# Linear attention times a gated layer, on one core: a key operand stored instead of formed late, two last stores moved to another queue, and small steps of the moments moved to ScalarE

## The chip, the cores and the metric

The kernel runs on one core of a Trainium2 chip. The metric is the device time in microseconds of one execution. The core has TensorE (PE; PEld is its weight load), VectorE (DVE), ScalarE (ACT), GpSimd (POOL) and SyncE (SP). In this kernel SyncE only issues transfers, and GpSimd issues transfers besides computing. Each engine works through its own queue in order; an instruction that waits holds everything behind it on its engine.

## The reference, cut to what matters

```python
xn = layernorm(x)                       # x: 2048 x 1024, eps 1e-5
q, k, v = split(xn @ wqkv)              # 32 heads of 32
phi = lambda t: where(t > 0, t + 1, exp(t)) + 1e-6
kv = einsum("hsd,hse->hde", phi(k), v);  z = sum_s phi(k)
o = (phi(q) @ kv) / (phi(q) @ z + 1e-6)
s = o @ wo
g = silu((silu(xn @ w1) * (xn @ w3)) @ w2)      # 1024 -> 3584 -> 1024
out = x + s * g
```

All of it is float32. The kernel never forms v. It forms the matrix xn^T phi(k), called G here, and multiplies that by the weights of v.

## The kernel before

**Products.** Every large product is cut into a 2 x 2 scheme with seven half-size products in place of eight, so each operand appears in seven forms: four quarters or less, and sums or differences of quarters (S1 to S4, T1 to T4). Each form is split in two parts, a high one (ScalarE, line 95) and the rest (VectorE, line 96), and each product of two forms is three matmuls (lines 103 to 105). A form therefore costs a pass of ScalarE and a pass of VectorE before TensorE can use it.

**The order.** `half(0)` and `half(1)` (lines 654 to 727) take 1024 rows of x each. A half normalises its rows and turns them into the seven left forms, then makes the keys (four pairs of 128 x 2 columns), the queries, and gate and up of the gated layer. After them come the attention product and the second product of the gated layer, in segments; the last segment finishes the output (`finish`, line 1191). The code is unrolled. A planner sets the order of the instructions on each engine from their order in the code, their operands' readiness and the free buffers by its own model of time; a few places hold it with `issue_after`, which puts instructions of a block behind a given one on that one's engine.

**The head of the first half.** The first chunk is 512 rows, four tiles of 128 x 1024 (`xa`). For each, `moments` (line 132) takes VectorE's batch statistics and `spread` (line 143) makes mean and 1/sqrt(variance + eps): one root on ScalarE, everything else in tiny VectorE steps of one or two columns. VectorE normalises the tile in place (line 157), and TensorE turns it. The second chunk (`xb`, line 191) has its moments two tiles at a time. For each of its tiles `prepare_rest` (line 201) normalises it on VectorE, then GpSimd forms S1, S3, S2 and S4 of both chunks, one after the other (lines 212 to 215), and stores them (line 217), and TensorE turns five forms, S2 and S4 from the first chunk's tile among them. The products T2 x S2 and after need the forms of all four tiles. Of the early key products, `gemm(..., early=True)` (line 432), only the two that need the quarters of the first chunk come before.

**The keys.** For each pair, `key_rows` (line 519) applies phi to the four quarters of the result; `turn` (line 532), called three steps of the surrounding products later, transposes them and forms the right operands Y00, Y01, Y10, R5, R4 and R2 of a later product, each 128 x 512, and stores them to DRAM (`keep_keys`, line 516, on GpSimd's queue). Y00, c21, c22, c12 and R2 come from one pool of six buffers (`small`, line 116).

**The row products.** In the second half, after its keys and queries, `row_products` (line 558) forms G: seven products, listed in `ROWS`, each summed over four pieces of 256 rows, so 28 steps. A step loads two tiles of x_d (SyncE, line 572) and two of y_d (line 570) into one of two `raw` buffers, splits them, and runs 24 matmuls. The seventh product needs R2 - Y00: it loads Y00 into an extra tile `yy` (from the four `job` buffers) and GpSimd subtracts it in place (line 583). The same `job` buffers serve side work that runs along: the denominators (line 841) and the division of the queries (`divide`, line 872, loads on lines 882 and 884).

**The end.** The last segment's `tokens` (line 1039) finish four quarters (t, n) of each of eight groups of 256 rows, in the order (1,1), (0,0), (1,0), (0,1). `finish` loads the factor s (and x), applies silu on ScalarE, multiplies, adds x and stores through GpSimd's queue. For rows with t = 1, except in the last group, the store adds to x in DRAM.

Of the kernel before, what the change touches and what calls it, by code (L numbers as in the profile page):

```python
# [16 lines left out]
P = 128  # L17
C = 512
# [4 lines left out]
def tile_linear_attention_times_swiglu(  # L23
# [32 lines left out]
    eps = const.tile([P, 1], F32, name="tiny")  # L56
    nc.vector.memset(eps, 1e-6)
    hmask = const.tile([P, P], F32, name="hmask")
    nc.vector.memset(hmask, 0.0)
# [24 lines left out]
    XS = ["A11", "A12", "S1", "S3", "A22", "S2", "S4"]  # L84
    YS = ["Y00", "Y01", "Y10", "R5", "R2", "R4"]
    x_d = [dram.tile([P, TH // 2, len(XS), C], F32, name=f"x_d{h}") for h in range(NH)]
# [44 lines left out]

    def moments(xs, dst):

        bs = st.tile([P, 2, 2, nc.vector.BN_STATS_DIM], F32, tag="bs", name="bs")
        for c, t in enumerate(xs):
            gather(t, bs[:, c])
        spread(bs, dst)

    def gather(t, bs):
# [3 lines left out]
    def spread(bs, dst):  # L143
        n = dst.shape[1]
        v, y, u = (st.tile([P, 2], F32, tag=a, name=a)[:, :n] for a in "vyu")
        for c in range(n):
            nc.vector.bn_aggr(out=dst[:, c], in_=bs[:, c])
        nc.vector.tensor_scalar_add(v, dst[:, :, 1], 1e-5)
        nc.scalar.activation(y, v, AF.Sqrt)
        nc.vector.reciprocal(y, y)  # L150

        nc.vector.tensor_mul(u, y, y)
        nc.vector.scalar_tensor_tensor(u, u, -0.5, v, op0=ALU.mult, op1=ALU.mult)
        nc.vector.scalar_tensor_tensor(dst[:, :, 1], u, 1.5, y, op0=ALU.add, op1=ALU.mult)

    def normalise(t, m):
# [19 lines left out]
    def prepare_first(A, mom):  # L176

        xs = []
        for g in range(TH // 4):
            t = load_rows([(2 * g + e) * P for e in range(2)], f"xa{g}")  # L180
            xs += [t[:, e] for e in range(2)]
            for i in (2 * g, 2 * g + 1):
                moments(xs[i:i + 1], mom[:, i:i + 1])
                normalise(xs[i], mom[:, i])
                keep_rows(0, i, "A11", xs[i])
                turn_into(A, {"A11": xs[i][:, :C]}, i, f"0_{i}")
        for i, t in enumerate(xs):
# [12 lines left out]

    def prepare_rest(A, mom, i, t0, seconds, behind):

        with ExitStack() as order:
# [4 lines left out]
            t1, s1 = seconds[i], small(f"S1x{i}")  # L208
            normalise(t1, mom[:, TH // 2 + i])

# [308 lines left out]
    def key_rows(h, pair):  # L519
# [12 lines left out]
        def turn(n, c, pk):  # L532
            V = nc.vector
            p_ = turned(pk, f"k{h}_{pair}_{n}{c}")
            if (c, n) == (0, 0):
                y00 = small(f"y00_{h}_{pair}")
                nc.scalar.activation(y00, p_, AF.Identity, bias=eps)  # L537
# [10 lines left out]
            else:  # L548
# [4 lines left out]
                for n_, t in (("Y01", y01), ("R4", r4), ("R2", r2)):  # L553
                    keep_keys(h, pair, n_, t)

        return use

    def row_products():
# [5 lines left out]
        def load(i, h, t):  # L564
            x_, y_, less = ROWS[i]
            raw = praw.tile([P, 4, C], F32, tag="raw", name=f"xy{i}_{h}{t}")

            def rows(dst, n):
                src = y_d[h][:, t:t + 2, YS.index(n)].rearrange("p t j d -> p t (j d)")
                nc.sync.dma_start(out=dst, in_=src)  # L570

            nc.sync.dma_start(out=raw[:, :2], in_=x_d[h][:, t:t + 2, XS.index(x_)])
            rows(raw[:, 2:], y_)
            other = None
            if less:
                other = job_tile([P, 2, C], f"yy{i}_{h}{t}")
                rows(other, less)
            return raw, other

        def ready(i, h, t):  # L580
            raw, other = data[i, h, t]
            if other is not None:
                nc.gpsimd.tensor_sub(out=raw[:, 2:], in0=raw[:, 2:], in1=other)
            out = []
            for e in range(2):
# [12 lines left out]
        for at, s in enumerate(steps):  # L598
# [25 lines left out]

    ROWS = [("A22", "Y10", None), ("A12", "Y00", None), ("S2", "R2", None), ("S1", "R4", None),
            ("S3", "R5", None), ("S4", "Y01", None), ("A11", "R2", "Y00")]

# [562 lines left out]

    def finish(m, t, n, a):
        r0, cols = (2 * m + t) * P, slice(n * C, (n + 1) * C)
        ss = small(f"ss{m}_{t}{n}")
        nc.sync.dma_start(out=ss, in_=s_d[2 * m + t][:, cols])
        if not added_by_dma(m, t):
            xs = small(f"xs{m}_{t}{n}")
            nc.sync.dma_start(out=xs, in_=x[r0:r0 + P, cols])
        nc.scalar.activation(a, a, AF.Silu)
        nc.vector.tensor_mul(a, a, ss)
        if not added_by_dma(m, t):  # L1200
            nc.vector.tensor_add(a, a, xs)
            nc.gpsimd.dma_start(out=out[r0:r0 + P, cols], in_=a)
        else:
# [98 lines left out]
```

## Time and profile before

| | us |
|---|---|
| median of 3 runs | 2360.43 (2357.89 to 2363.99) |
| the profiled execution, its own time | 2364.7 |
| its span, first to last instruction | 2362.9 |
| TensorE busy in the span | 2306.2 |
| VectorE, ScalarE, GpSimd busy | 1775.7, 924.5, 697.2 |
| mean granted TensorE clock | 0.992 |

The execution's own time is 1.8 us more than its span; this lies around the first and last instruction. A row of a timeline gives start, duration, engine, line, operation, output and inputs, how many were merged, and in brackets the idle time of the engine before it with what ended it. A row of the waits gives who waited, for whom, the total in us, how often, and the longest. A row of the windows gives the stretch, its length, the busy us of PE, PEld, DVE, ACT and POOL with the number of instructions, the granted clock, the DMA share and GB/s. `SPq` and `POOLq` are the issue of a transfer or a wait in that engine's queue.

### The profile page before, as it was taken

How to read it: one execution, taken by the hardware profiler on the slowest of the kernel's cores; microseconds unless marked ns; L12 is line 12 of the kernel's file. 1: busy time of each engine (PE TensorE's matmuls, PEld its weight loads, DVE VectorE, ACT ScalarE, POOL GpSimd, SP SyncE). 2: the span in 40 equal slices, each digit the busy share in tenths (PEclk: the TensorE clock that was granted, in tenths of full speed). 3: DMA queues.
4: the chain of work that ended last, by engine and by line, in shares of the span. 5: the costliest groups of instructions: out<-in, count | busy, mean ns of one | idle time of the engine just before them, and what ended most of it. 6: DMA issues, size and time to landing. Idle time of an engine off the chain costs nothing.

```text
span 2362.9 us, 30966 instructions
## 1 busy us (share of the span) xinstructions
PE 2306.2 (98%) x10368; PEld 1893.2 (80%) x10368; DVE 1775.7 (75%) x2822; ACT 924.5 (39%) x1639; POOL 697.2 (30%) x852
## 2 busy tenths in 40 slices
PE   6999999999999999998999999999999999999998
PEld 5788878888887888776888888888887788888876
DVE  8887888898877775656867688887745666767798
ACT  5555343423232555433233332334324534342433
POOL 5120433377866111012423435342310000000033
PEclk9999999999999999999999999999999999999999
DMA  6555455576669546776665567665756565766688
GB/s 236 165 174 178 156 179 183 172 228 220 225 210 321 196 134 205 255 257 207 201 193 181 188 200 218 195 216 168 230 153 195 181 198 172 225 208 182 191 265 260
DMA packets 354015, 479.69 MB, mean 203 GB/s; under 512 B 24144, under 2 KB 262736, under 8 KB 353744
## 3 DMA queue, kind: packets, MB, share of 16 engines
q1 hardware_dynamic: 316608, 359.20, 48.1%
q0 software_dynamic: 37248, 118.52, 15.2%
q8 instruction: 81, 1.33, 0.2%
q14 instruction: 78, 0.64, 0.1%
HBM read 308.81 MB, written 172.49 MB: 204 GB/s over the span
## 4 chain that ended last, share of the span: by engine, by line
PE 74%; DMA 5%; DVE 5%; issue 2%; ACT 1%; SPq 1%; POOL 0%; DVEq 0%; POOLq 0%; ACTq 0%
PE g L103 2%; PE g L104 2%; PE g L105 2%; PE cB L103 1%; PE cB L104 1%; PE cB L105 1%; PE dB L103 1%; PE dB L104 1%; PE dB L105 1%; PE aB L105 1%; PE aB L103 1%; PE aB L104 1%; DMA rA12B<-h_d 1%; PE bB L105 1%; PE bB L103 1%
## 5 line engine op out<-in xcount | busy, mean ns | idle before, releaser
L756 POOL DMA_DIRECT2D h_d<-sg x112 | 82.7, 739 | 262.5 <-DVE sg L752 183.9
L1069 POOL DMA_DIRECT2D u_d<-uB x32 | 17.3, 541 | 407.9 <-DVE uB L1052 354.8
L96 DVE TENSOR_TENSOR xy<-xy,xy 128x512 fp32r<-128x512 f32 x112 | 75.0, 704 | 70.4 <-ACT xy L95 70.2
L95 ACT CAST xy<-xy 128x512 fp32r<-128x512 f32 x112 | 65.1, 620 | 109.3 <-PE g L105 62.5
L103 PE MATMUL g<-xy,xy 128*128 128x512 f32 x224 | 82.3, 403 | 7.1 <-ACT xy L95 7.1
L104 PE MATMUL g<-xy,xy 128*128 128x512 f32 x224 | 88.5, 395 | 0.0
L105 PE MATMUL g<-xy,xy 128*128 128x512 f32 x224 | 87.9, 393 | 0.0
L517 POOL DMA_DIRECT2D y_d<-y x40 | 28.6, 718 | 141.9 <-ACT y L537 81.6
L1052 DVE TENSOR_TENSOR acc<-cB,acc 128x512 f32<-128x512 f32 x50 | 34.4, 688 | 40.2 <-PE cB L105 40.2
L1052 DVE TENSOR_TENSOR acc<-dB,acc 128x512 f32<-128x512 f32 x56 | 38.5, 688 | 31.0 <-PE dB L105 30.8
L736 POOL TENSOR_TENSOR hs<-hs,sg 128x256 f32<-128x256 f32 x56 | 61.1, 1090 | 0.1
L103 PEld LDWEIGHTS g<-xy,xy 128*128 128x128 f32 x224 | 42.1, 190 | 21.9 <-ACT xy L95 9.6
L738 POOL TENSOR_TENSOR hs<-sg 128x256 f32<-128x256 f32 x56 | 57.7, 1031 | 0.0
L894 POOL DMA_DIRECT2D qs_d<-qd x32 | 18.0, 564 | 119.3 <-DVE qd L890 82.0
L1183 POOL DMA_DIRECT2D s_d<-s x32 | 17.3, 541 | 117.7 <-DVE s L1052 70.9
L735 POOL TENSOR_TENSOR hs<-sg,sg 128x256 f32<-128x256 f32 x56 | 50.8, 906 | 1.2
L104 PEld LDWEIGHTS g<-xy,xy 128*128 128x128 f32 x224 | 42.7, 190 | 9.9 <-issue 0.8
L739 POOL TENSOR_TENSOR hs<-sg,hs 128x256 f32<-128x256 f32 x56 | 49.9, 892 | 1.5
L105 PEld LDWEIGHTS g<-xy,xy 128*128 128x128 f32 x224 | 42.6, 190 | 9.2
L771 POOL TENSOR_TENSOR w<-w 128x256 f32<-128x256 f32 x28 | 28.2, 1006 | 70.9 <-DMA w<-in_B_w 69.7
L764 POOL DMA_DIRECT2D h_d<-hs x60 | 45.8, 765 | 4.3 <-POOL hs L739 2.4
L674 POOL DMA_DIRECT2D pq_d<-pq x32 | 17.5, 546 | 91.1 <-DVE pq L507 88.3
(5315 smaller groups left out, 8330.1 us busy)
## 6 DMA issues: line engine op xcount, KB each, us to landing
h_d<-hs POOLq DMA_DIRECT2D x60, 256.0 KB, 3.5
h_d<-sg POOLq DMA_DIRECT2D x56, 256.0 KB, 3.9
w<-in_B_w SPq DMA_DIRECT2D x56, 256.0 KB
wt_d<-w SPq DMA_DIRECT2D x28, 512.0 KB
xy<-x_d SPq DMA_DIRECT2D x28, 512.0 KB
xy<-y_d SPq DMA_DIRECT2D x28, 512.0 KB
h_d<-hs SPq DMA_DIRECT2D x52, 256.0 KB
qs_d<-qd POOLq DMA_DIRECT2D x32, 384.0 KB, 3.9
```

The source lines that it names most:

```text
L95: nc.scalar.copy(out=hi, in_=src)
L96: return nc.vector.tensor_sub(out=lo, in0=src, in1=hi.bitcast(F32))
L103: nc.tensor.matmul(acc, lhsT=wh, rhs=ah, start=start, stop=False, skip_group_check=True)
L104: nc.tensor.matmul(acc, lhsT=wh, rhs=al, start=False, stop=False, skip_group_check=True)
L105: return nc.tensor.matmul(acc, lhsT=wl, rhs=ah, start=False, stop=stop, skip_group_check=True)
L735: e.tensor_add(out=s1, in0=a21, in1=a22)
L736: e.tensor_sub(out=s2, in0=s1, in1=a11)
L738: e.tensor_sub(out=s3, in0=a11, in1=a21)
L739: e.tensor_sub(out=s4, in0=a12, in1=s2)
L756: nc.gpsimd.dma_start(out=h_d[i][2 * h + c][:, 2 * n:4 * n + 2, k], in_=src)
L764: queue.dma_start(out=h_d[i][2 * h + c][:, 6 + 4 * e:10 + 4 * e, k], in_=o[e].rearrange("p (e s) -> p e s", s=P))
L1052: return V.tensor_add(out=c, in0=src, in1=c)
```

## The change

It has three parts.

1. In `key_rows`, Y00's tile is kept; when R2 is formed, VectorE overwrites it with R6 = R2 - Y00, and it is stored as a seventh key operand. `ROWS` names R6 for the seventh product; the `yy` load and GpSimd's subtraction go.
2. In the last group of rows, the stores of (1,0) and (0,1) are issued by SyncE, the others by GpSimd as before. A new `fetch` holds the loads of `finish`; in the last group the loads for (0,1) are issued with those of (1,0), ahead of its store.
3. In the first half, each tile has moments of its own (`settle`). VectorE keeps the statistics, their aggregate and the reciprocal; ScalarE makes the one-column steps: six with the root for a tile of the first chunk, eight for one of the second, where it also forms minus mean times the scale, and then normalises the tile in one pass. The first chunk's tiles are still normalised by VectorE, and the second half's rows are left as they are.

```diff
+    few = const.tile([P, 2], F32, name="few")
+    nc.vector.memset(few[:, 0:1], 1e-5)
+    nc.vector.memset(few[:, 1:2], 1.5)
...
-    YS = ["Y00", "Y01", "Y10", "R5", "R2", "R4"]
+    YS = ["Y00", "Y01", "Y10", "R5", "R2", "R4", "R6"]
...
+    def settle(bs, m, shift):
+        v, y, u = (st.tile([P, 2], F32, tag=a, name=a) for a in "vyu")
+        def act(out, src, **how):
+            nc.scalar.activation(out, src, AF.Identity, **how)
+        mean, r = m[:, 0:1], m[:, 1:2]
+        nc.vector.bn_aggr(out=m, in_=bs)
+        act(v[:, :1], r, bias=few[:, 0:1])
+        nc.scalar.activation(y[:, :1], r, AF.Sqrt, bias=few[:, 0:1])
+        nc.vector.reciprocal(y[:, :1], y[:, :1])
+        act(u[:, :1], y[:, :1], scale=y[:, :1])
+        act(u[:, :1], u[:, :1], scale=v[:, :1])
+        act(u[:, :1], u[:, :1], scale=-0.5, bias=few[:, 1:2])
+        act(r, u[:, :1], scale=y[:, :1])
+        if shift:
+            act(u[:, 1:], mean, scale=r)
+            act(mean, u[:, 1:], scale=-1.0)
...
-                moments(xs[i:i + 1], mom[:, i:i + 1])
+                bs = st.tile([P, 2, nc.vector.BN_STATS_DIM], F32, tag="bs", name="bs")
+                gather(xs[i], bs)
+                settle(bs, mom[:, i], False)
                 normalise(xs[i], mom[:, i])
...
-        moments(ts, mom[:, j:j + 2])
+        for e, t in enumerate(ts):
+            bs = st.tile([P, 2, nc.vector.BN_STATS_DIM], F32, tag="bs", name="bs")
+            gather(t, bs)
+            settle(bs, mom[:, j + e], True)
...
-            normalise(t1, mom[:, TH // 2 + i])
+            m1 = mom[:, TH // 2 + i]
+            nc.scalar.activation(t1, t1, AF.Identity, scale=m1[:, 1:2], bias=m1[:, 0:1])
...
-                y00 = small(f"y00_{h}_{pair}")
+                y00 = rows["y00"] = small(f"y00_{h}_{pair}")
...
+                V.tensor_sub(out=rows["y00"], in0=r2, in1=rows["y00"])
+                keep_keys(h, pair, "R6", rows["y00"])
...
-            other = None
-            if less:
-                other = job_tile([P, 2, C], f"yy{i}_{h}{t}")
-                rows(other, less)
-            return raw, other
+            return raw
...
-            if other is not None:
-                nc.gpsimd.tensor_sub(out=raw[:, 2:], in0=raw[:, 2:], in1=other)
...
-            ("S3", "R5", None), ("S4", "Y01", None), ("A11", "R2", "Y00")]
+    ROWS = [("A22", "Y10"), ("A12", "Y00"), ("S2", "R2"), ("S1", "R4"), ("S3", "R5"), ("S4", "Y01"), ("A11", "R6")]
...
+    factors = {}
+    def fetch(m, t, n):
         r0, cols = (2 * m + t) * P, slice(n * C, (n + 1) * C)
-        ss = small(f"ss{m}_{t}{n}")
+        ss, xs = small(f"ss{m}_{t}{n}"), None
         nc.sync.dma_start(out=ss, in_=s_d[2 * m + t][:, cols])
         if not added_by_dma(m, t):
             xs = small(f"xs{m}_{t}{n}")
             nc.sync.dma_start(out=xs, in_=x[r0:r0 + P, cols])
+        factors[m, t, n] = ss, xs
+
+    def finish(m, t, n, a):
+        r0, cols = (2 * m + t) * P, slice(n * C, (n + 1) * C)
+        if (m, t, n) not in factors:
+            fetch(m, t, n)
+        if (m, t, n) == (NG - 1, 1, 0):
+            fetch(m, 0, 1)
+        ss, xs = factors[m, t, n]
+        queue = nc.sync if m == NG - 1 and t != n else nc.gpsimd
         nc.scalar.activation(a, a, AF.Silu)
         nc.vector.tensor_mul(a, a, ss)
         if not added_by_dma(m, t):
             nc.vector.tensor_add(a, a, xs)
-            nc.gpsimd.dma_start(out=out[r0:r0 + P, cols], in_=a)
+            queue.dma_start(out=out[r0:r0 + P, cols], in_=a)
```

More of the change, by code (lines that the diff above doesn't have):

```diff
@@ L130, in load_rows @@
         return t
[L132 to L137, printed above, removed]
     def gather(t, bs):
@@ L564, in load @@
         def load(i, h, t):
-            x_, y_, less = ROWS[i]
+            x_, y_ = ROWS[i]
             raw = praw.tile([P, 4, C], F32, tag="raw", name=f"xy{i}_{h}{t}")
@@ L573, in load @@
             rows(raw[:, 2:], y_)
-            other = None
-            if less:
-                other = job_tile([P, 2, C], f"yy{i}_{h}{t}")
-                rows(other, less)
-            return raw, other
+            return raw
         def ready(i, h, t):
-            raw, other = data[i, h, t]
-            if other is not None:
-                nc.gpsimd.tensor_sub(out=raw[:, 2:], in0=raw[:, 2:], in1=other)
-            out = []
+            raw, out = data[i, h, t], []
             for e in range(2):
@@ L623, in row_products @@
             del data[s]
-    ROWS = [("A22", "Y10", None), ("A12", "Y00", None), ("S2", "R2", None), ("S1", "R4", None),
-            ("S3", "R5", None), ("S4", "Y01", None), ("A11", "R2", "Y00")]
+    ROWS = [("A22", "Y10"), ("A12", "Y00"), ("S2", "R2"), ("S1", "R4"), ("S3", "R5"), ("S4", "Y01"), ("A11", "R6")]
     def row_sums(i, m, b, u, v):
@@ L1189, in added_by_dma @@
         return m < ADDED and t == 1
-    def finish(m, t, n, a):
+    factors = {}
+    def fetch(m, t, n):
         r0, cols = (2 * m + t) * P, slice(n * C, (n + 1) * C)
-        ss = small(f"ss{m}_{t}{n}")
+        ss, xs = small(f"ss{m}_{t}{n}"), None
         nc.sync.dma_start(out=ss, in_=s_d[2 * m + t][:, cols])
```

## The prediction

> **What bounds the kernel now.** I read the page's busy shares first, then the list of who waits for whom on TensorE, then the table of windows, then the timelines of the places that the waits point to.
>
> ```profile
> PE 2306.2 (98%) x10368; PEld 1893.2 (80%) x10368; DVE 1775.7 (75%) x2822; ACT 924.5 (39%) x1639; POOL 697.2 (30%) x852
> ...
> PE tA L164 <- DVE v L148: 11.2, 1, 11.2
> PE g L103 <- ACT xy L95: 7.1, 2, 6.9
> PE bk__735 L103 <- ACT S L95: 4.7, 1, 4.7
> PE tS L164 <- DVE pk L507: 2.9, 1, 2.9
> ...
> 40.00:50.00 10.00, 5.70 (x30) 4.70 (x28) 9.96 (x13) 4.53 (x9) 9.89 (x11) 0.80 0.49 200
> ...
> 1080.00:1090.00 10.00, 4.34 (x10) 3.47 (x11) 2.59 (x4) 2.28 (x4) 2.33 (x1) 0.68 0.73 204
> ```
>
> TensorE is busy 98% of the span (first row), so what can be won is where it stands still. The rows of waits give engine, what was awaited, us in total, times, longest. The long ones lie in two places that the change touches: the head (11.2, 4.7, 2.9) and one step of the row products (6.9). The window rows give PE, PEld, DVE, ACT, POOL busy of 10 us, then the granted clock, which falls to 0.80 and 0.68 just there: a pause is paid twice, once as idle time and once as slow matmuls behind it. Outside these places TensorE never stops for long, so microseconds won there should reach the end.
>
> **Part 1, R2 - Y00 stored as R6.** The last four of the 28 steps of the row products lose a 512 KB load and a GpSimd subtraction each. The last step is the one that TensorE waited for:
>
> ```profile
> 1067.34 3.25 SPq L884 DMA_DIRECT2D qd<-pq_d  x1
> ...
> 1072.40 1.07 SPq L570 DMA_DIRECT2D xy<-y_d  x1
> ...
> 1082.63 2.33 POOL L583 TENSOR_TENSOR xy<-xy,yy 128x1024 f32<-128x1024 f32 x1 [8.67 <-DMA xy<-y_d]
> ...
> 1085.66 2.07 PE L103 MATMUL g<-xy,xy 128*128 128x512 f32 x4 [6.87 <-ACT xy L95]
> ...
> 1093.48 0.39 PE L103 MATMUL ag__9096<-A,B11g__9047 128*128 128x512 f32 x1
> 1093.71 0.39 PE L104 MATMUL ag__9096<-A,B11g__9047 128*128 128x512 f32 x1
> ...
> SPq L882 <- POOL xy L583: 3.8, 1, 3.8
> ...
> y_d<-r POOLq DMA_DIRECT2D x8, 256.0 KB, 3.4
> ```
>
> The chain reads backwards: TensorE starts the step at 1085.66 after 6.87 us, because GpSimd subtracts for 2.33 us from 1082.63, because the keys issued at 1072.40 land only then, 10 us later. That issue is late since SyncE's queue holds loads of the division (L882, L884) ahead of it, which in turn waited 3.8 us for the subtraction to give back `job` buffers, and those loads share the DMA engines with it. The step's 24 matmuls take 1085.66 to 1093.48, 7.82 us; at the 0.23 us between the two rows of `ag` they take 5.5. So the stall costs 6.87 + 2.3 = 9.2 us.
>
> With R6 stored no `yy` holds a `job` buffer, so the division's loads go out earlier, as the denominators' four free up, ahead of the last step's loads. Four loads of 512 KB are gone, though the division's take part of that room. The last step's `raw` buffer comes free when the step two before it is split, which waits for no subtraction any more. If only the 3.25 us of L884 go ahead of them, the keys are issued at 1069.2; landing in 7 us (an estimate between the 3.4 that a store of half the size takes, last row, and the 10.2 here) they are there at 1076.2, and the first operand 0.7 us later (1082.63 + 2.33 to 1085.66), before 1078.79, where TensorE stood still. I take -9.2. Bounds: -10.2, if the weight behind it comes earlier too, and -2.3, if the loads stay late and only the subtraction goes.
>
> What R6 adds is eight subtractions and eight 256 KB stores, one per key pair:
>
> ```profile
> 101.25 0.68 DVE L507 SCALAR_TENSOR_TENSOR pk<-c12k__1007,pk 128x512 f32<-128x512 f32 x1
> ...
> 103.13 0.68 DVE L552 SCALAR_TENSOR_TENSOR r<-trk,y 128x512 f32<-128x512 f32 x1
> ...
> 125.43 0.81 POOL L517 DMA_DIRECT2D y_d<-r  x1
> ...
> 100.00:120.00 20.00, 20.00 (x101) 16.57 (x100) 17.09 (x35) 11.47 (x21) 5.75 (x8) 1.00 0.52 159
> ```
>
> Eight times 0.68 is 5.4 us of VectorE and eight times 0.81 is 6.5 of GpSimd. In the key windows VectorE has 2.9 us in 20 free and GpSimd 14, and TensorE never pauses, so this hides; uncovered it would be 5.4. There is a new wait: R6 overwrites Y00's tile, so VectorE must wait until Y00's store has read it; behind it in VectorE's queue stand the additions of the next product. Two products lie between (24 matmuls, 5.5 us), and a store takes 0.8 + 3.4. And Y00's tile stays held. In the first half four pairs make Y00 early, the last at:
>
> ```profile
> 88.86 0.68 ACT L537 ACTIVATE y<-trk,tiny 128x512 f32<-128x512 f32 x1
> ```
>
> From there to about 108 (R2's row, 0.8 to issue and 3.4 to land after it), four of the six small buffers are Y00s, and c22, c21, c12 and R2 live on two. By their rows they overlap by at most two (c12 is read by 101.9, R2 is born at 103.1, the first two rows), so it just fits. I put +1.0 for both (0 to 5.4).
>
> **Part 2, the head.** For the second chunk VectorE makes moments and normalises while GpSimd sums:
>
> ```profile
> 21.24 3.65 DVE L141 BATCH_NORM_STATS2 bs<-xb 128x6 f32<-128x512 f32 x6
> ...
> 28.25 0.16 DVE L153 SCALAR_TENSOR_TENSOR u<-u,v 128x2 f32<-128x2 f32 x1
> ...
> 30.79 1.52 DVE L157 TENSOR_SCALAR xb<-xb,mom 128x1024 f32<-128x1024 f32 x2
> ...
> 36.92 2.81 DVE L154 SCALAR_TENSOR_TENSOR mom<-u,y 128x2 f32<-128x2 f32 x1
> 39.77 4.30 DVE L157 TENSOR_SCALAR xb<-xb,mom 128x1024 f32<-128x1024 f32 x2
> ...
> 31.68 1.79 POOL L212 TENSOR_TENSOR S1x<-xb 128x512 f32<-128x512 f32 x1 [15.08 <-DVE xb L157]
> ...
> 57.54 1.30 POOL L215 TENSOR_TENSOR xa<-xa 128x512 f32<-128x512 f32 x1
> ...
> 57.09 0.66 PE L164 MATMUL tS<-ident,xa 128*128 128x128 f32 x4 [0.69 <-POOL xa L214]
> ...
> 62.62 0.62 ACT L95 CAST T2k__721<-wk__714 128x512 fp32r<-128x512 f32 x1 [2.51 <-DVE wk__714 L346]
> ...
> 63.66 0.58 ACT L95 CAST S<-tS 128x512 fp32r<-128x512 f32 x1
> 64.29 0.80 PE L103 MATMUL bk__735<-S,T2k__721 128*128 128x512 f32 x1 [4.74 <-ACT S L95]
> ```
>
> A normalisation takes 0.76 us before GpSimd begins and 2.15 with GpSimd at work, and a step of two columns goes from 0.16 to 2.81. GpSimd's chain starts when the first tile is normalised (31.68) and runs without a gap to 58.8; the product T2 x S2 needs its last tile, and then waits for a cast that ScalarE makes at 63.66, behind weight splits that VectorE delivered late.
>
> The new path of the first tile, by these rows:
>
> ```profile
> 27.62 0.20 ACT L149 ACTIVATE y<-v 128x2 f32<-128x2 f32 x1 [1.34 <-DVE v L148]
> ...
> 33.26 1.28 ACT L149 ACT_TABLE_LOAD   x1
> ...
> 92.04 0.58 ACT L541 COPY y<-trk 128x512 f32<-128x512 f32 x1
> ...
> 20.00:40.00 20.00, 19.29 (x96) 15.96 (x95) 17.28 (x35) 13.04 (x22) 8.20 (x8) 1.00 0.36 127
> ```
>
> Its statistics are done near 22.5, a third into the six of 21.24. Then ScalarE makes eight small steps, whose nearest row is `y<-v`, 0.20 us; a tile as an operand adds 0.10 (0.68 with `tiny`, 0.58 for the copy), so seven of 0.30 and one of 0.20 make 2.3. With VectorE's aggregate and reciprocal and eight hand-offs I estimate 3.1. The normalisation, from 0.20 for two columns and 0.62 for 512, is 1.05 for 1024, and 1.25 with two tile operands. That is 26.9. In ScalarE's queue two copies and two weight casts stand in that stretch, 2.4 us, and perhaps a wait for a weight: 2.8. So GpSimd starts near 29.7 instead of 31.7: -2.0, bounds -4.5 (nothing in between) and +3 (the next tile's steps first). VectorE loses at least the 8.6 us of the three long rows, so that the 2.9 us wait for `pk` and part of the 7.2 us between the last transposes (57.09) and 64.29 go: -3.0, bounds 0 and -5.5. The first chunk's steps move too, where VectorE is full; I put 0 (-1 to +1.5). The head: -5.0.
>
> A rule speaks against this part. The Trainium skill ("ScalarE: Activation LUTs", Rules for kernel authors) says to do adds and multiplies on VectorE, not on ScalarE. By it these steps get longer, and the head would gain nothing or lose; by the rows above, the rule's VectorE time is not what VectorE takes beside a working GpSimd.
>
> **Part 3, the tail.**
>
> ```profile
> 2352.94 0.54 POOL L1202 DMA_DIRECT2D out<-acc  x1 [1.23 <-DVE acc L1201]
> ...
> 2356.13 1.14 POOL L1202 DMA_DIRECT2D out<-acc  x2 [2.65 <-DVE acc L1201]
> ...
> L1298 POOLq DRAIN  x3: 45/93/5453, 2356.7 to 2362.7; - x3
> ...
> DMA to landing us min/median/max: 2.3/5.9/6.7
> ...
> SPq L1298 <- PEq L1298: 2.9, 2, 2.4
> ```
>
> The last two stores stand one behind the other on GpSimd, and then GpSimd's drain takes 5.45 us from 2356.71 to 2362.16; SyncE, done with the stores, waits 2.4 us more for the others. With these stores on SyncE, GpSimd's last one is that of 2352.94 and its drain, if as long, ends at 2358.9. SyncE issues its last store no later than GpSimd did (2356.7); with the fastest landing shown, 2.3, and 0.4 for the waits, it is done at 2359.4, 2.8 us before 2362.16. That is -2.8 (bounds -3.3 and 0). The factors' early loads only stop SyncE's queue from holding them behind a store. The Trainium skill ("DMA: Bandwidth & Descriptors", Issuing engines are not separate DMA queues) says that another issuer saves only its sequencer's time, usually little. By that rule the tail would give some 0.3, by the drain's row 2.8.
>
> **The sum:** -9.2 + 1.0 - 5.0 - 2.8 = -16.0 on the profiled execution's 2364.7 us, so 2348.7 for a profiled run. The median of the runs, 2360.43, is 4.3 lower, and I predict on it: 2344.4.
>
> **The rivals.**
> - *ScalarE takes the head's wait over.* It was busy 13.0 of the 20 us from 20 to 40 and gets four tiles of 3.5 us more (2.3 and 1.25). Against it: GpSimd takes some 6.8 us for each tile (four in 27.1), so the last two are due much later. Head 0: -11.0, 2349.4. It is where the ScalarE page's rule would lead.
> - *The row products' stall stays*, because the division's loads take the place of the keys: for it speaks that SyncE's queue is in order; against it, that those loads are limited by four buffers. Only 2.3 go: -9.1, 2351.3. With the first rival as well: -4.1, 2356.3.
> - *Slower:* all of ScalarE's added work, 14 us, and two more pairs of table loads of 1.28 us, should each root now stand alone between exponentials (5.1), lie ahead of GpSimd's chain. Head +19, the rest -11: +8, 2368.4. It turns the sign once more than 11 us lie there. Against it: the first two roots are due before the first exponential.
>
> **How the numbers follow.** Forecast 0.50, ScalarE bound 0.19, stall stays 0.13, both 0.09, slower 0.09. The range takes the forecast's best end (head -10, row products -10.2, tail -3.3: 2337) and reaches to the case of both at 2356.3 with a little beyond it, 2358. A measurement of this kernel can tell 0.3%, 7.1 us, from no change; that puts the border at 2353.3. The forecast and most of the two single rivals lie under it, 0.74; both, and the late ends of these, within, 0.18; slower 0.08.
>
> **What would show it.** Right: no `yy`, the last step of `g` starts without a wait and the clock from 1070 to 1090 stays near 1.0; GpSimd's first sum starts before 31 and the T2 product before 60; the long drain of GpSimd ends before SyncE's. Wrong: waits of VectorE for stores at R6, waits for small buffers between 89 and 145, table loads of ScalarE before GpSimd's first sum.

## The result and the profile after

The changed kernel takes 2349.52 us (median of 6 runs, 2346.09 to 2352.79); the kernel before took 2364.52 us in the 6 runs beside them (2357.89 to 2368.56). The ratio is 0.9939, 95% interval 0.9920 to 0.9957, so 10 to 19 us were won. The profiled execution of the changed kernel took 2352.79 us, the slowest of its six, with a span of 2351.0 and a granted clock of 0.995; against the profiled execution before that is 11.9 us.

Where these 11.9 us come from is read off five landmarks of the timelines. Only starts that stand in both traces are compared; each stretch runs from one landmark to the next.

| from, to | before | after | change |
|---|---|---|---|
| start to the first T2 x S2 product (`bk`) | 64.29 | 63.73 | -0.6 |
| to the first matmul of the row products (`g`) | 853.35 | 851.34 | -2.0 |
| to the first matmul after them (`ag`) | 175.84 | 167.21 | -8.6 |
| to VectorE's last pair of additions | 1261.67 | 1261.87 | +0.2 |
| to the end of the span | 7.75 | 6.85 | -0.9 |

The list of waits of the changed kernel, with engine, what was awaited, us in total, times and the longest:

```profile
PE tA L180 <- DVE y L163: 11.7, 1, 11.7
PE tS L180 <- POOL xa L236: 7.9, 3, 4.2
...
PE bk__774 L106 <- ACT S L98: 1.6, 1, 1.6
...
PE g L106 <- ACT xy L98: 0.8, 1, 0.8
```

The 6.9 us wait of `g` is down to 0.8. The head's waits have mostly changed their names: 4.7 for `bk` became 1.6, 2.9 for `pk` went, and those for GpSimd's `xa` grew from 1.4 to 7.9. Between 20 and 70 us TensorE waits 10.5 us in all, where it was 11.1.

The timeline of the changed kernel at the last step of the row products, and rows of its windows:

```profile
915.07 0.39 PE L106 MATMUL g<-xy,xy 128*128 128x512 f32 x1
...
1058.05 0.41 SPq L594 DMA_DIRECT2D xy<-y_d  x1
...
1064.73 0.47 SPq L594 DMA_DIRECT2D xy<-y_d  x1
...
1076.19 0.51 PE L106 MATMUL g<-xy,xy 128*128 128x512 f32 x1 [0.82 <-ACT xy L98]
...
1082.28 0.39 PE L106 MATMUL ag__9139<-A,B11g__9090 128*128 128x512 f32 x1
```

```profile
30.00:40.00 10.00, 7.71 (x37) 6.33 (x36) 1.38 (x7) 9.94 (x25) 6.02 (x6) 0.94 0.13 52
...
1070.00:1080.00 10.00, 8.96 (x38) 6.87 (x37) 4.29 (x8) 2.90 (x5) 0.00 (x0) 1.00 0.58 192
1080.00:1090.00 10.00, 10.00 (x46) 8.27 (x45) 8.50 (x14) 4.54 (x8) 2.16 (x4) 1.00 0.53 193
```

The last step's keys are asked for at 1064.73 instead of 1072.40, TensorE runs the step 9.5 us earlier (2.6 of them were won ahead of `g`) with a wait of 0.82, and the clock stays at 1.00, where it had been 0.68. The first row is the head: from 30 to 40 us ScalarE (the fourth of the busy times) is full with 9.94 of 10 us and VectorE is down to 1.38. The same stretch before:

```profile
30.00:40.00 10.00, 9.29 (x52) 7.70 (x51) 8.64 (x14) 7.46 (x13) 8.20 (x8) 1.00 0.20 79
```

VectorE's time is freed there, 8.64 us down to 1.38, but the product behind it comes only 0.6 us earlier.

The head in the timeline of the changed kernel:

```profile
21.57 2.46 DVE L137 BATCH_NORM_STATS2 bs<-xb 128x6 f32<-128x512 f32 x4
23.95 0.20 DVE L160 BATCH_NORM_AGGREGATE mom<-bs 128x2 f32<-128x12 f32 x1
...
24.18 0.29 ACT L157 ACTIVATE v<-mom,few 128x1 f32<-128x1 f32 x1 [0.84 <-DVE mom L160]
...
29.58 1.28 ACT L528 ACT_TABLE_LOAD   x1
30.88 0.63 ACT L528 ACTIVATE pk<-pk 128x512 f32<-128x512 f32 x1
...
32.53 1.24 ACT L231 ACTIVATE xb<-xb,mom 128x1024 f32<-128x1024 f32 x1
...
33.85 1.29 POOL L234 TENSOR_TENSOR S1x<-xb 128x512 f32<-128x512 f32 x1 [16.65 <-ACT xb L231]
...
46.75 1.29 POOL L234 TENSOR_TENSOR S1x<-xb 128x512 f32<-128x512 f32 x1
47.98 0.57 POOL L190 DMA_DIRECT2D x_d<-xa  x1
...
51.11 0.37 SPq L348 DMA_DIRECT2D wk__753<-in_A_wqkv  x1
...
58.39 0.66 PE L180 MATMUL tS<-ident,xa 128*128 128x128 f32 x4 [4.17 <-POOL xa L236]
...
62.06 0.62 ACT L98 CAST T2k__760<-wk__753 128x512 fp32r<-128x512 f32 x1 [2.51 <-DVE wk__753 L368]
...
63.11 0.58 ACT L98 CAST S<-tS 128x512 fp32r<-128x512 f32 x1
63.73 0.50 PE L106 MATMUL bk__774<-S,T2k__760 128*128 128x512 f32 x1 [1.61 <-ACT S L98]
```

GpSimd's first sum starts at 33.85, 2.2 us later than before. The rows from 46.75 on play a part below.

The end, from the timeline, the instructions of the exit line (L1326; a row gives how many, the shortest, median and longest in ns, and the first and last start), and SyncE's waits:

```profile
2341.93 0.54 POOL L1230 DMA_DIRECT2D out<-acc  x1 [1.23 <-DVE acc L1229]
...
2344.15 1.29 DVE L1229 TENSOR_TENSOR acc<-acc,xs 128x512 f32<-128x512 f32 x2
2344.86 0.94 SPq L1230 DMA_DIRECT2D out<-acc  x2
```

```profile
L1326 POOLq DRAIN  x3: 45/93/8312, 2341.9 to 2350.7; - x3
L1326 SPq DRAIN  x3: 7/7/13, 2347.9 to 2350.5; - x3
```

```profile
SPq L1326 <- PEq L1326: 2.9, 2, 2.4
...
SPq L1326 <- DMA out<-acc: 1.5, 2, 0.9
```

SyncE has its last store landed at 2347.9, 3.8 us after the pair of additions began. GpSimd issues its last transfer at 2341.93, yet the drain that begins there takes 8.31 us, where it had taken 5.45, and SyncE waits 2.4 us for the others exactly as before.

### The profile page after: what moved, and what is told of

It is laid out like the page before. It is cut to its first block, busy times and chain, and to the rows that moved or that the text cites. A ratio compares the mean times of both kernels' runs of the same rounds, so it can differ in the third digit from the quotient of the medians.

```text
span 2351.0 us, 31018 instructions
## 1 busy us (share of the span) xinstructions
PE 2301.9 (98%) x10368; PEld 1891.8 (80%) x10368; DVE 1768.3 (75%) x2806; ACT 940.0 (40%) x1694; POOL 688.7 (29%) x854
## 4 chain that ended last, share of the span: by engine, by line
PE 60%; issue 9%; DVE 4%; DMA 4%; POOL 2%; ACT 1%; SPq 0%; DVEq 0%; POOLq 0%; ACTq 0%
PE g L106 2%; PE g L107 2%; PE g L108 2%; PE cB L106 1%; PE dB L108 1%; PE cB L108 1%; PE dB L106 1%; PE cB L107 1%; PE dB L107 1%; PE aB L108 1%; PE aB L106 1%; PE aB L107 1%; POOL s_d L1199 1%; PE bB L108 1%; PE bB L107 1%
## 5 line engine op out<-in xcount | busy, mean ns | idle before, releaser
L539 POOL DMA_DIRECT2D y_d<-y x48 | 34.6, 720 | 138.2 <-ACT y L559 77.7
L98 ACT CAST XS4B<-rS4B 128x384 fp32r<-128x384 f32 (+1 forms) x40 | 19.7, 493 | 59.3 <-PE cB L108 41.1
```

What stands on the lines that cost most here:

```text
L98: nc.scalar.copy(out=hi, in_=src)
```

## The experiments

Eleven kernels ran. Ratios are against the kernel before, from runs on the same chip; the runs of the kernel before had medians of 2364.37 us beside the first four, 2364.26 beside the next four and 2366.51 beside the last three.

| kernel | us | ratio (95%) | first sum | `wk` asked | `bk` | `g` to `ag` | last additions to end | GpSimd's drain |
|---|---|---|---|---|---|---|---|---|
| before | 2364.52 | 1 | 31.68 | 50.28 | 64.29 | 175.84 | 7.75 | 5.45 |
| changed | 2349.52 | 0.9939 (0.9920-0.9957) | 33.85 | 51.11 | 63.73 | 167.21 | 6.85 | 8.31 |
| e1, R6 only | 2350.60 | 0.9949 (0.9936-0.9962) | 32.48 | 51.10 | 65.05 | 166.14 | 10.85 | 8.48 |
| e2, head only | 2363.12 | 0.9997 (0.9988-1.0005) | 35.21 | 52.46 | 65.08 | 174.89 | 7.79 | 5.45 |
| e3, tail only | 2360.41 | 0.9984 (0.9974-0.9993) | 31.98 | 50.09 | 63.28 | 176.41 | 4.33 | 5.29 |
| e4, head split | 2344.04 | 0.9916 (0.9903-0.9929) | 29.62 | 49.60 | 63.28 | 166.10 | 6.85 | 8.31 |
| e5, load kept | 2358.67 | 0.9975 (0.9964-0.9987) | 33.92 | 51.16 | 63.80 | 175.02 | 6.79 | 8.31 |
| e6, subtraction kept | 2350.39 | 0.9939 (0.9926-0.9953) | 35.32 | 52.56 | 65.19 | 169.17 | 6.81 | 8.31 |
| e7, four stores on SyncE | 2347.29 | 0.9931 (0.9918-0.9944) | 35.06 | 52.29 | 64.93 | 167.19 | 4.56 | 9.26 |
| e8, head stores on SyncE | 2341.59 | 0.9907 (0.9891-0.9923) | 34.03 | 47.91 | 60.31 | 165.84 | 5.26 | 6.68 |
| e9, e4 and e8 | 2344.19 | 0.9908 (0.9893-0.9923) | 28.98 | 46.46 | 60.04 | 165.79 | 5.22 | 6.68 |
| e10, R6's stores on SyncE | 2348.31 | 0.9927 (0.9911-0.9944) | 34.26 | 51.52 | 64.16 | 165.74 | 4.61 | 5.29 |
| e11, e9 and e7 | 2342.43 | 0.9900 (0.9885-0.9914) | 29.66 | 47.15 | 60.72 | 166.08 | 4.78 | 8.18 |

`wk` is the first key's second weight, asked for by SyncE. The columns behind the ratio are of one profiled execution each. The expectations count the tail from the last addition of a product, which starts 2.0 us before the pair used in this table, so 9.7 and 8.8 there are 7.75 and 6.85 here.

### One part at a time

**e1, R6 only.** The kernel before with `Y00` overwritten by R6, stored, and named in `ROWS`; head and tail as before.

> The kernel before with part 1 alone (R6 stored, the yy load and the subtraction gone). Theory: nearly all of the gain is the stall of the last row product's step. The first gate product after it (1093.48 before, 1082.28 with all three parts) starts 8 to 10 us earlier than before, the T2 x S2 product of the head stays within 0.3 us of 64.29, the time falls by 8 to 10 us. Rival: part 1 needs the head's earlier start, or hides part of its cost there; then the gate product comes less than 6 us earlier, and the time falls by 3 to 6.

**e2, head only.** The kernel before with `settle` and ScalarE's normalisation.

> The kernel before with part 3 alone (moments on ScalarE). Theory: ScalarE has taken the wait over. GpSimd's first sum starts near 33.9 instead of 31.7, the T2 x S2 product 0.3 to 1 us before 64.29, and the time moves by less than 2 us. Rival: with R6's stores absent the head is worth the 5 us that were forecast, because the small buffers that Y00 holds cost it in the full change; then the stretch from 64 to 122 us gets shorter than 58.1 us by 2 or more, and the time falls by 3 to 6.

**e3, tail only.** The kernel before with the two stores on SyncE and `fetch`.

> The kernel before with part 2 alone (the two last stores and the early factors). Theory: GpSimd's long drain does not wait for GpSimd's own stores but ends some 2.4 us after SyncE has seen the last landing, whoever issued it; so the stretch from the last addition of a product (2353.16 before) to the end of the span shrinks by 0.7 to 1.1 us, and the rest stays. Rival: the drain is GpSimd's own; the stretch shrinks by 2.5 to 3.3 us.

R6 alone gives 12.1 us by its ratio (0.0051 x 2364), more than the 8 to 10 that were expected, and shortens the row products by 9.7 (175.84 to 166.14); in its profile the tail is 3.1 us longer (10.85 against 7.75), so it gives something back at a place that it doesn't touch. The head alone gives nothing that can be measured; its first sum comes at 35.21 and its product at 65.08, later than expected and later than before. The tail alone gives 3.8 us, 3.4 of them at the end of the profiled execution, so the drain is GpSimd's own (the rival) and does not end 2.4 us behind SyncE whoever stores. By their ratios the three parts add up to 16.6 us against 14.4 together. The intervals are wider than this difference, but the profiles have one of that size in the tail, 3.4 us alone and 0.9 with the rest. The drains of e1 and of e3, each from the instructions of its exit line:

```profile
L1300 POOLq DRAIN  x3: 45/93/8475, 2343.9 to 2352.9; - x3
```

```profile
L1310 POOLq DRAIN  x3: 45/93/5290, 2352.7 to 2359.1; - x3
```

With the tail's edit alone the drain takes 5.29 us from 2352.7 and is over before SyncE's store has landed, as the prediction had it. With R6 alone it takes 8.48. So the 3.0 us by which the drain is longer come with R6, and without R6 the tail's edit has its full effect.

### Where the stall in the row products came from

**e5** brings back the load and its buffer, without the subtraction:

```diff
+            other = None
+            if y_ == "R6":
+                other = job_tile([P, 2, C], f"yy{i}_{h}{t}")
+                rows(other, "Y00")
...
+                nc.gpsimd.tensor_copy(out=other[:, 0, :1], in_=other[:, 1, C - 1:])
```

> The changed kernel, but the four last steps of each half's row products fetch Y00 again as well (512 KB into a job buffer, given back by a GpSimd copy of one column); nothing is subtracted, and the values computed are those of the changed kernel. Theory 1, the stall came from the load and the buffer that it held, which kept the division's loads behind it in SyncE's queue and so the last step's own loads late: the last step waits again for some us, the stretch from the first matmul of g to that of ag is 172 to 176 us (167.2 in the changed kernel, 175.9 before), time 2354 to 2358. Theory 2, the stall came from GpSimd's subtraction ahead of the split: the stretch stays at 167 to 168.5, time 2348.5 to 2351.

**e6** brings back a subtraction of the same size, without the load. It subtracts the rows of x_d that lie beside the keys, since Y00 is not loaded; the seventh product is then another one than the reference's:

```diff
+            if ROWS[i][1] == "R6":
+                nc.gpsimd.tensor_sub(out=raw[:, 2:], in0=raw[:, 2:], in1=raw[:, :2])
```

> The changed kernel, but GpSimd makes a subtraction of the same size as before (128x1024) on the loaded keys of those steps, from the rows loaded beside them; no load is added. The seventh product's second operand is another one than the reference's. Theory 1 (the load and its buffer): the subtraction of 2.3 us lies in the 10 us that the loads now have in hand, the stretch from g to ag stays at 167 to 169, time 2348.5 to 2351. Theory 2 (the subtraction): 171 to 176, time 2353 to 2358.

The load brings nearly all of it back: 175.02 us from `g` to `ag`, and the ratio goes from 0.9939 to 0.9975, 8.5 us. It is the last step but one that waits, not the last. The list of waits, the timeline and the windows of e5:

```profile
PE g L106 <- ACT xy L98: 7.2, 1, 7.2
...
SPq L594 <- DMA yy<-y_d: 8.4, 2, 7.7
...
SPq L904 <- DMA yy<-y_d: 4.7, 1, 4.7
```

```profile
1059.04 2.03 SPq L904 DMA_DIRECT2D qd<-r_d  x1
...
1065.77 0.91 SPq L594 DMA_DIRECT2D xy<-y_d  x1
...
1076.72 2.08 PE L106 MATMUL g<-xy,xy 128*128 128x512 f32 x4 [7.20 <-ACT xy L98]
```

```profile
1070.00:1080.00 10.00, 3.28 (x8) 2.60 (x9) 2.59 (x4) 2.28 (x4) 0.00 (x0) 0.66 0.73 215
```

SyncE's queue is in order. Loads on L594 and one of the division (L904) wait 8.4 and 4.7 us for a `job` buffer that a `yy` holds; when it comes back, the division's loads (L904, L906) go out in a row, and the keys of the step stand behind them, at 1065.77, where the changed kernel asks for the same step's keys at 1058.05. TensorE waits 7.20 us, and the clock falls to 0.66 in that stretch. A one-column copy is all that GpSimd does there, so the subtraction isn't needed for the stall.

The subtraction alone costs 2.0 us in the stretch (169.17 against 167.21), at two steps that wait 0.95 and 2.05 us, and nothing in the ratio. Theory 1 had allowed up to 169. So of the stall the load with its buffer is nearly 8 us, and the subtraction at most 2; with both, in the kernel before, the stretch is 175.84. The time of e5, 2358.67, lies just above the 2358 that its theory allowed.

### What the drain hangs on

**e7** puts all four stores of the last group on SyncE:

```diff
-        queue = nc.sync if m == NG - 1 and t != n else nc.gpsimd
+        queue = nc.sync if m == NG - 1 else nc.gpsimd
```

> The changed kernel with all four stores of the last group on SyncE, two more than now, so that GpSimd issues 468 transfers in all (470 now, 472 with the row products' part alone, 464 before, 462 with the tail's part alone; its last drain took 8.31, 8.48, 5.45 and 5.29 us there). Theory 1, the drain's length goes by the number of transfers that GpSimd issued, 0.08 us each in a pair's difference, and it starts behind its last one: it takes 8.15 us, starts near 2338 and ends before SyncE's own last store has landed; from VectorE's last addition to the end 6.3 to 6.8 us (8.8 now), time 2346.5 to 2348. Theory 2, the drain ends 2.4 us behind SyncE's first one whatever GpSimd issued: 8.8 us as now, time 2349 to 2351.

**e8** puts the head's twelve stores of S1, S3 and S2 on SyncE. It also asks what sets the first T2 x S2 product, taken up in the next section:

```diff
+        by_sync = h == 0 and n != "A11"
-        nc.gpsimd.dma_start(out=x_d[h][:, i, e:e + k], in_=t.rearrange("p (n c) -> p n c", c=C))
+        (nc.sync if by_sync else nc.gpsimd).dma_start(out=x_d[h][:, i, e:e + k], in_=t.rearrange("p (n c) -> p n c", c=C))
```

> The changed kernel with the head's twelve stores of the first half's sums (S1, S3 and S2 of four tiles) issued by SyncE instead of GpSimd. Two things are tried at once, each with its own landmark. First, the drain: 458 transfers on GpSimd, under the 464 of before; if its length goes by their number it takes 4.6 to 5.0 us instead of 8.31, and from VectorE's last addition to the end are 6.3 to 6.8 us instead of 8.8. If it doesn't, 8.3 and 8.8 stay. Second, the head: theory A, the T2 x S2 product starts when the first key's second weight has come, whose load waits for the second tile's S2 store (issued 47.98, load issued 51.11), which stands in GpSimd's queue behind the third tile's first sum: the load goes out near 47.3, GpSimd's chain ends near 54.5 instead of 60.2, the product starts at 60 to 61 instead of 63.7. Theory B, it is ScalarE's and VectorE's queue of casts, whatever the load: 63 to 64. With the drain and A 2342 to 2345; with the drain alone 2346.5 to 2348; with neither 2349 to 2351.

**e10** leaves everything as in the changed kernel but R6's eight stores, which go to SyncE:

```diff
+        (nc.sync if n == "R6" else nc.gpsimd).dma_start(out=y_d[h][:, :, YS.index(n), pair], ...)
```

> The changed kernel with R6's eight stores issued by SyncE instead of GpSimd, so that GpSimd's list of transfers is the one of the tail's part alone (462). Theory 1, the length of GpSimd's last drain is a property of that list: 5.29 us, as with the tail's part alone, it ends before SyncE's own store has landed, 2.4 us less behind VectorE's last addition than now, time 2346.5 to 2348.5, if SyncE's queue loses nothing by the eight stores. Theory 2, the drain is longer for another reason that came with R6 (its keys' longer lives, or the order of the work): 8.31 us and 8.8 us of tail stay, time 2349 to 2351. If R6's stores hold up the loads behind them in SyncE's queue, it is slower than this in either, and the weights' loads between 89 and 150 show it.

The drains of e7, e8 and e10, from the instructions of each one's exit line:

```profile
L1326 POOLq DRAIN  x3: 45/93/9259, 2336.2 to 2348.7; - x3
```

```profile
L1327 POOLq DRAIN  x3: 45/102/6678, 2336.0 to 2343.2; - x3
```

```profile
L1326 POOLq DRAIN  x3: 45/102/5293, 2341.0 to 2347.6; - x3
```

The theory that its length goes by the number of GpSimd's transfers falls: with 458 of them (e8) it takes 6.68 us, longer than the 5.45 with 464 (before), and with 468 (e7) 9.26, longer than the 8.31 with 470. The theory that it ends 2.4 us behind SyncE whatever GpSimd issued falls as well: in e7 and e10 SyncE waits at most 0.5 us for the others. What stands is that the length belongs to GpSimd's list of transfers. Kernels with the same list have it to within 4 ns, wherever the time went before: 5.453 before and in e2; 8.312 in the changed kernel, e4, e5 and e6; 5.290 in e3 and 5.293 in e10, whose lists are alike; 6.678 in e8 and 6.682 in e9. R6's eight stores, hundreds of microseconds before the end, are what makes it 8.31: with them on SyncE it is 5.29 again, the tail is 2.2 us shorter (6.85 to 4.61), and the time, 2348.31, lies in the range that was expected; the ratio, 0.9927, has an interval that overlaps the changed kernel's, so the 2.2 us rest on the profiles. By which rule a list gives its length stays open. SyncE's queue lost nothing that can be seen by those stores: `bk` to `g` takes 850.8 us (851.3).

The Trainium skill ("DMA: Bandwidth & Descriptors", Issuing engines are not separate DMA queues) says that another issuer saves only its sequencer's time, usually little. Here the measurement decides against it: at the end of the kernel the tail's edit alone saved 3.4 us, since GpSimd's drain, the last thing to end before, then starts 3.8 us earlier, seen from the last additions.

### What sets the head

**e4** gives the first two tiles of the second chunk back to VectorE, moments and normalisation, and holds them ahead of the other tiles' statistics and of the first key's phi with `issue_after`; ScalarE keeps the last two tiles:

```diff
+            if 2 * g + e in (0, 1):
+                spread(bs.rearrange("p (c k) s -> p c k s", c=1), mom[:, j + e:j + e + 1])
+            else:
+                settle(bs, mom[:, j + e], True)
...
+            if i in (0, 1):
+                done.append(normalise(t1, m1))
+            else:
+                nc.scalar.activation(t1, t1, AF.Identity, scale=m1[:, 1:2], bias=m1[:, 0:1])
...
+        if i in (0, 1):
+            behind.append(done[-1])
...
+            with tc.issue_after(done[-1].ins):
+                next(m[0])
+                next(m[1])
```

> All three parts, but for the first two tiles of the second chunk VectorE keeps the moments and the normalisation, one tile at a time and ahead of the third and fourth tile's statistics and of the first key's phi; ScalarE keeps the last two tiles, which fall due while GpSimd sums. Theory: what the head is worth is set by when GpSimd's chain starts. It starts near 28.5 instead of 33.9, the T2 x S2 product near 59 instead of 63.7, and the time falls by 3 to 6 us against the full change. Rival: the weight of the first T products, or the casts behind the chain, set the product's start; then GpSimd starts earlier by 5 us and the product by less than 1.5.

GpSimd's first sum comes 4.2 us earlier (29.62), but the product only 0.45 us (63.28). So the product does not follow GpSimd's first sum, though the prediction let it. What it hangs on stands in SyncE's waits. The longest of the changed kernel from 20 to 70 us:

```profile
SPq L348 <- DMA x_d<-xa: 25.2, 1, 25.2
...
```

The load of `wk` waits for a `raw` buffer that the first chunk's first two tiles hold until the second tile's S2 is stored. That store (47.98 in the timeline above) stands on GpSimd behind the third tile's first sum (46.75). It lands, the load goes out at 51.11, VectorE forms T2, and its split starts at 62.06, after ScalarE has waited 2.51 us for VectorE. The left form was there before: its last pieces are turned at 58.39, and its cast (63.11) stands on ScalarE behind that of T2.

This also says where e4 lost its lead. The timeline of e4:

```profile
45.24 1.29 POOL L242 TENSOR_TENSOR S1x<-xb 128x512 f32<-128x512 f32 x1 [2.10 <-ACT xb L239]
46.48 0.57 POOL L190 DMA_DIRECT2D x_d<-xa  x1
...
49.60 0.37 SPq L358 DMA_DIRECT2D wk__747<-in_A_wqkv  x1
```

GpSimd stands still for 2.10 us until ScalarE has normalised the third tile, so the store behind that tile's first sum is only 1.5 us earlier, and so is the load. From the load's issue to the product e4 then takes 13.7 us, the changed kernel 12.6. By the table this stretch is 12.62 to 12.64 in each of the six kernels that leave all these tiles to ScalarE and the head's stores to GpSimd, and 13.2 to 14.0 where VectorE keeps the first two or all of them: VectorE's freed time is worth about 1 us there, and GpSimd's later start took part of it back (the load goes out 0.8 us later than before).

e8 takes the store out of GpSimd's queue; its timeline:

```profile
47.91 0.38 SPq L349 DMA_DIRECT2D wk__753<-in_A_wqkv  x1
...
54.10 1.28 POOL L238 TENSOR_TENSOR xa<-xa 128x512 f32<-128x512 f32 x1
...
60.31 0.79 PE L106 MATMUL bk__774<-S,T2k__760 128*128 128x512 f32 x1 [3.83 <-ACT T2k__760 L98]
```

The load goes out 3.2 us earlier, and the product starts 3.4 us earlier, while GpSimd's first sum is where it was (34.03). That is theory A. e8 alone does not separate the weight from GpSimd's chain, whose last sum starts 4.8 us earlier as well (54.10 instead of 58.85); that the weight comes last is read from the waits, here 3.83 us of TensorE for T2. With the tail's 1.6 us the profiled execution wins 5.0 us up to here; the ratio, 0.9907, says 7.6 against the changed kernel, with intervals that just touch.

**e9** does both, e4's split and e8's stores; **e11** has e7's four stores as well.

> The kernel with the head split (the first two tiles of the second chunk on VectorE, 2344.04 us) and its twelve head stores issued by SyncE. Theory 1, the two add up: GpSimd's first sum stays near 29.6, the first key's second weight is asked for near 46.6 (49.60 with the split alone, 47.91 with the stores moved alone), the T2 x S2 product starts at 59 to 60, from VectorE's last addition to the end are 1.5 us less than with the split alone, time 2336 to 2340. Theory 2, past 60.3 the splits of the weight on VectorE and ScalarE set the product whatever came earlier: it starts at 60 to 61 as with the stores moved alone, and only the tail's 1.5 us and the split's gain behind the head remain: 2340 to 2343. In both GpSimd's drain takes 6.68 us, if its length is fixed by GpSimd's list of transfers.

> The head split, the twelve head stores on SyncE, and all four stores of the last group on SyncE as well. With all four there the tail was 0.8 us shorter than with the twelve moved, so this should be 0.5 to 1 us faster than the same kernel with two of the four; GpSimd's drain has begun near 7 us before VectorE's last addition and may take 9 us unseen. Theory 1 of the kernel beside it: 2335 to 2339; theory 2: 2339 to 2342.

They don't add up. The weight is asked for at 46.46 in e9, the product starts at 60.04: 1.45 us won at the load are 0.27 at the product. The waits of e9 from 20 to 66 us, and its timeline, name what has taken over:

```profile
POOL S1x L243 <- ACT xb L240: 4.4, 1, 4.4
...
ACT T2k__754 L98 <- DVE wk__747 L379: 2.0, 1, 2.0
PEld bk__768 L106 <- ACT T2k__754 L98: 2.0, 1, 2.0
```

```profile
40.26 0.32 SPq L191 DMA_DIRECT2D x_d<-xa  x1
45.92 0.32 SPq L191 DMA_DIRECT2D x_d<-S1x  x1
46.46 0.38 SPq L359 DMA_DIRECT2D wk__747<-in_A_wqkv  x1
```

VectorE forms T2 between its splits, ScalarE waits for it, and TensorE for ScalarE: theory 2. There is a second hold: the second tile's S2 is stored at 40.26, but the weight's load stands in SyncE's queue behind the third tile's S1 store (45.92), whose sum waits 4.4 us for ScalarE's normalisation. e9's own time, 2344.19, lies above the range of both theories, and so does e11's, 2342.43; e9's ratio, 0.9908, is that of e8. e11 has the lowest ratio, 0.9900, and is the only one whose interval lies clear of the changed kernel's (0.9920 to 0.9957); those of e8 and e9 end at 0.9923, that of e4 at 0.9929. By their middle values the four are 5 to 9 us faster than the changed kernel, and among themselves they can't be told apart. The gain of e4 over the changed kernel arises bit by bit behind the head (-0.45 at `bk`, -4.8 at `g`, -5.9 at `ag`, -9.2 at the last additions); no single wait explains it, and it wasn't followed up. Its time fits the 3 to 6 us that its first theory gave, but its head is that of the rival, so the theory isn't borne out by it.

## Why the prediction was right, and where not

The forecast was 2344.4 us, the measured time 2349.52, inside the range and faster as said. What happened in the head is the first rival's case. That the time meets its 2349.4 is chance: on the base of the six runs the forecast would be 2348.5, and that rival 2353.5. By size the forecast's -16.0 stands against -15.0 between the medians (-14.4 by the ratio). The other 4.1 of the 5.1 us lie in the base: 2360.43 was the median of three runs, and with three more it is 2364.52. That the sum came so near is in part luck. In the profiled pair, 11.9 us apart, the head and the tail gave 1.5 of their 7.8; 2.0 came between the head and the row products, where only a cost was forecast, and some 3 us are the distance of that pair from the medians.

- **The row products' stall, -9.2: right, -8.6.** The mechanism was the one given, the queue of SyncE with the `yy` loads and buffers in it; e5 brings 7.8 of it back with the load alone, and e6 shows 2.0 for the subtraction, where the prediction's lower bound had 2.3 for it. The second rival, that the division's loads take the keys' place, is what e5 shows with the `yy` load and what the changed kernel doesn't show.
- **R6's added work, +1.0: right at its place, and missed elsewhere.** The eight subtractions take 0.68 to 0.69 us each, VectorE never stood idle ahead of one, and TensorE's only wait between 85 and 150 us is one of 0.2 us for another tile. But the eight stores on GpSimd made its drain 3.0 us longer at the other end of the kernel (e1, e10). The prediction counted their 0.81 us each and called it hidden; this part of the cost it did not have.
- **The head, -5.0: wrong, -0.6 at the product and nothing in e2.** The step that failed is "so GpSimd starts near 29.7". It started at 33.85. The single steps had their estimated size: 0.28 to 0.30 us for a small one, 1.24 for a normalisation (1.25). What was wrong is what stood between them. The first tile's aggregate waits on VectorE for the second tile's statistics (23.95; half of the merged row of 21.57 is over near 22.8), and from there to its normalisation 8.4 us pass on ScalarE (24.18 to 32.53) instead of 3.1 + 2.8, since the planner put the other tiles' steps, two weight casts, two copies and the first key's phi with its table load of 1.28 us in between, and VectorE's reciprocal for it comes only at 26.49. That is the first rival, ScalarE takes the wait over. In e4, with the first two tiles on VectorE and ahead of that phi, the sum starts at 29.62; e4 does not separate the engine from the order. The second failed step is that VectorE's freed time was to pull the product forward by 3.0 us. It was freed (1.38 us busy of 10) and is worth some 1.4 us between the weight's load and the product (14.01 and 12.62), but the product waits for a weight whose load waits for a store in GpSimd's queue, behind the third tile's sum (e4, e8). The prediction had that load in no term, and no rival had it.
- **ScalarE's rule.** The Trainium skill ("ScalarE: Activation LUTs", Rules for kernel authors) says to do adds and multiplies on VectorE, and budgets some 0.3 us for an instruction. The 0.3 us agrees: 0.28 to 0.30 for the small steps. A head that gains nothing (e2, ratio 0.9997) is what the rule would lead to, but it doesn't show the rule's reason, since the product waits for the weight's load. The same table budgets about 2.7 us for a switch of tables; here the load takes 1.28 us, and the next activation starts 1.30 us after the load has begun (29.58, 30.88).
- **The slower rival** did not come: one table load more than before stands in the first 66 us, not two pairs. It stands in the first chunk, at 6.37, where TensorE's longest wait grows from 11.2 to 11.7.
- **The tail, -2.8: the mechanism right, the size -0.9.** Alone it gives 3.4 us in the profile and 3.8 by the ratio (e3). In the changed kernel the term "its drain, if as long" failed: 8.31 us instead of 5.45, because of R6's stores (e10), so it ended behind SyncE's stores and not before them.
- **Open:** the 2.0 us between the first T2 x S2 product and the row products. Kernels with the same code up to there reach `g` at 913.42 (e6) to 917.50 (e7), so much of it is spread between executions.

## What to carry to other kernels

When a stage waits at a product, follow each of its operands back to the transfer that brings it, and that transfer back to whoever gives its buffer free; work moved off a busy engine wins only what reaches that chain: here 7 us of freed VectorE time were 0.6 at the product. Extra loads cost most, in this kernel, through the in-order queue and the buffers that they hold (7.8 us), less through the arithmetic that uses them (2.0 or less). And a store added on GpSimd anywhere in a kernel may have to be paid at its end, in GpSimd's drain, when nothing else is left to hide it.

## What the runs showed of the hardware that was not expected

GpSimd's drain at the end of the program is long and stays the same to within 4 ns for the same list of transfers: 5.29, 5.45, 6.68, 8.18, 8.31, 8.48 and 9.26 us in these kernels, with 462, 464, 458, 456, 470, 472 and 468 transfers. Two stores less at the end shorten it by 0.163 us (before and e3; e1 and the changed kernel), eight stores more long before it lengthen it by 3.02. It does not grow with the number: two stores less than in the changed kernel make it 9.26 (e7), twelve less 6.68 (e8). It overlaps whatever the other engines still do, so it costs only what sticks out behind SyncE's last landing.
